# Scores of eleven query blocks in 64x64 tiles instead of 64x32, with new orders for all engines

## The chip, the cores and the metric

The kernel runs on one core of one Trainium2 chip. The metric is the device time of one execution in microseconds (us). TensorE is called PE in the profile (PEld are its weight loads), VectorE is DVE, ScalarE is ACT, GpSimd is POOL and SyncE, which issues the DMAs, is SP.

## What is computed

Four residual layers over a sequence of 2048 tokens of width 448, in bfloat16. Layers 0 and 2 are attention, layers 1 and 3 a gated product. Each attention query looks at eight keys: its own position and the seven positions 2, 4, ..., 14 back.

```python
# layers 0 and 2: 16 heads of 28
q, k, v = split((layernorm(x) @ wqkv))
logits  = sum(q[s] * k[s - 2*w]) * 28**-0.5      # w = 0..7, masked before position 0
x = x + softmax(logits) @ v-window @ wo
# layers 1 and 3: F = 1792
h = layernorm(x)
x = x + ((h @ w_gate) * (h @ w_up)) @ w_down
```

## The kernel before

**Tokens and layout.** Even and odd tokens never meet in the attention, so x is kept with all even tokens first, and the window of eight keys becomes eight neighbours. A head of 28 is padded to 32 rows. All large products run in mode R64 (`MAIN`): PE is cut into two halves of 64 rows, and two products, one in each half, run beside each other (the 64\*128 tiles of the profile).

**Attention.** The queries are cut into 17 blocks: block 0 of 128 queries, the others of 120. Block 0 is a group by itself, the other blocks go two by two, so there are nine groups, g = 0..8, per attention layer. For each group `attn_front` (line 811) does these steps. DVE writes Qz (line 820), two copies of the queries, each with half of the heads set to zero. PE computes the scores S in one burst (line 832): keys are stationary, queries move. A burst of a pair of blocks has 64 products: 4 chunks of heads x 2 blocks x 2 halves of the keys (c) x 2 strips of 32 keys (s\_) x 2 halves of the rows (p). Each loads 32 keys, and streams two copies of 32 or 40 queries. That is mode C32 (`BURST`): tiles of 64 rows by 32 columns, eight of them at once. Then ACT takes the exponential (line 841) in two instructions and DVE masks by a minimum (line 848). `attn_back` (line 852) multiplies by v in a second burst AV, also 64 products of mode C32 (line 866); ACT and DVE evict it (877, 881), `norm` divides (891 to 904), and `y_blocks` multiplies by wo and adds to x (921).

**Gated layers.** `b_chunk` (line 931) takes chunks of 256 or 512 tokens: for each of 14 slices of F a unit of 14 products (G and U of a slice beside each other), ACT copies G (957), DVE multiplies it by U into hT (960), and 14 + 14 products with WD add to x (921). The last 256 tokens use whole-array products (line 972) and smaller adds (976).

**What sets the order.** The program is a list of 1593 operations with dependencies; no planner runs. `ORDER` gives the order of the operations on each engine as literal numbers, and `BANKS` gives the PSUM banks of each PE operation. In the PE list, `548*3/418` means that burst 548 is cut into four pieces, and between the pieces the first three product pairs of operation 418 run as strips of 32 columns (line 351), which is the burst's own mode, so that PE need not change mode for them; a burst that is a number alone stands alone. `24+25/26` puts two bursts ahead of one host. Where ACT, DVE and POOL can do the same copy, the list in which its number stands decides. In `crossed` (line 632) a product group is done in two parts, with the row halves exchanged; the second part waits for the end of the first on PE itself, so the lists normally put other work between the two parts (373 and 374, for example, are the two parts of one v group).

The score bursts are 215 (g 0), 249, 271, 379, 401, 526, 548, 599, 621 in layer 0, and 765 to 1355 in layer 2. The AV bursts are 220, 254, 276, 384, 406, 531, 553, 604, 626, and 770 to 1360.

Of the kernel before, what the change touches and what calls it, by code (L numbers as in the profile page):

```python
# [12 lines left out]
W = 8  # L13
# [15 lines left out]
BURST = "C32"  # L29
MAXALT = 3  # L30
# [63 lines left out]
def grp_nc(g):  # L94
# [21 lines left out]
    ),  # L116
    "act": (
# [12 lines left out]
    ),  # L130
    "dve": (
# [18 lines left out]
    ),  # L150
    "pool": (
        "22 23 24 39 40 18 32 33 25 19 20 28 21 41 42 44 29 26 27 34 35 64 67 68 65 71 73 74 76 36 37 30 43 31 38"
    ),
# [185 lines left out]
def pe_cols(n):  # L339
    return n / 2.4 + 2.6  # L340
# [36 lines left out]
def build(nc, A_x, A_wqkv, A_wo, B_w_gate, B_w_up, B_w_down, out):  # L377
# [22 lines left out]
    qk = sb([128, 2, 4, S], bf, "qk")  # L400
# [11 lines left out]
    Qz = sb([128, NZ, 2, 4, 2 * QB], bf, "Qz")  # L412
# [8 lines left out]
    ps = enter(nc.psum_tensor("ps", [128, 8, 512], dt.float32))  # L421

    sc = Sched()
# [121 lines left out]
    for n in range(4):  # L545
        a, z = 7 * n // 2, 7 * (n + 1) // 2
# [264 lines left out]
    def attn_front(li, g, prio):  # L811
        qbs, nc = grp_qbs(g), grp_nc(g)
        nd = len(qbs)
# [289 lines left out]
```

## Time and profile before

| | |
|---|---|
| three runs | 389.02, 389.04, 389.85 us (median 389.04) |
| profiled execution, whole | 389.22 us |
| its span from first to last instruction | 387.4 us |
| granted PE clock | 0.999 |
| PE busy | 378.5 us, 6442 products and as many weight loads |
| DVE / ACT / POOL busy | 290.9 / 203.1 / 9.2 us |
| L832 (scores), 64\*32 tiles | 1088 products, 89 ns a load, 185 to 208 ns a product by the record |
| L866 (times v), 64\*32 tiles | 1088 products |

A line of the timeline gives the start, the length from the first start to the last end, the engine and source line, out<-in, the PE tile (rows\*columns), the shape and the count; brackets give idle time before it and what ended it. A product's record goes on for some 0.19 us after its operands have been issued, since products are pipelined. So the cost of a group is read from its start to the start of the next group, not from its length. The whole time of the profiled execution is 1.8 us longer than the span: that lies before the first and behind the last instruction.

### The profile page before, as it was taken

To read this page: it belongs to the slowest core of one execution; us is meant where nothing else is said; L and a number is where in the kernel's file an instruction comes from. 1 tells how busy PE (TensorE), PEld (TensorE's weight loads), DVE (VectorE), ACT (ScalarE), POOL (GpSimd) and SP (SyncE) were. 2 spreads that over 40 slices of the span, in tenths; PEclk is the share of its full clock that TensorE was granted. 3 is DMA by queue.
4 is the path that set the end of the run, shared out by engine and by line. 5 is a ranking of instruction groups with operands and counts; after the bars stand their busy time and mean duration, and the time that the engine had idled before them with its cause. 6 is when DMAs were issued, how large, how long until landed. Compare 5 with 4: busy or idle time off the path is not lost.

```text
span 387.4 us, 14498 instructions
## 1 busy us (share of the span) xinstructions
PE 378.5 (98%) x6442; PEld 213.2 (55%) x6442; DVE 290.9 (75%) x643; ACT 203.1 (52%) x386; POOL 9.2 (2%) x39
## 2 busy tenths in 40 slices
PE   7999899999999999999999999999999999999996
PEld 3655468644455544555656667654555544445763
DVE  7988899999974877597877788667997877365332
ACT  5999787565634643355364535446655643044310
POOL 6020000000000000000000000000000000000000
PEclk9999999999999999999999999999999999999999
DMA  7765641800502060122022204300133005030002
GB/s 263 181 159 135 100 116 47 104 12 12 88 17 52 3 96 15 24 44 47 17 31 51 42 2 96 70 14 5 49 48 72 2 2 98 13 83 2 3 25 85
DMA packets 54882, 22.52 MB, mean 58 GB/s; under 512 B 45012, under 2 KB 54820, under 8 KB 54820
## 3 DMA queue, kind: packets, MB, share of 16 engines
q1 hardware_dynamic: 54676, 21.53, 26.7%
q8 instruction: 51, 0.84, 0.9%
q14 instruction: 11, 0.09, 0.1%
q10 hardware_dynamic: 144, 0.06, 0.1%
HBM read 8.54 MB, written 2.71 MB: 29 GB/s over the span
## 4 chain that ended last, share of the span: by engine, by line
PE 93%; DVE 2%; ACT 1%; DMA 1%; SPq 1%; issue 1%; DVEq 0%
PE ps L348 84%; PE ps L351 2%; PE ps L866 2%; PE ps L832 2%; PE ps L972 1%; DMA hT<-in_A_wqkv_dram 1%; ACT E_sb L841 1%; SPq L441 1%; PE ps L614 0%; DVE x_sb L921 0%; DVE hT L960 0%; DVE E_sb L848 0%; ACT g_sb L957 0%; DVE qk L709 0%; DVEq L1052 0%
## 5 line engine op out<-in xcount | busy, mean ns | idle before, releaser
L348 PE MATMUL ps<-xnTb,WGU 64*128 64x512 bf16 (+1 forms) x1926 | 175.5, 333 | 1.0 <-ACT E_sb L841 0.4
L348 PEld LDWEIGHTS ps<-xnTb,WGU 64*128 64x128 bf16 x1926 | 94.0, 94 | 72.3 <-issue 2.3
L957 ACT ACTIVATE g_sb<-ps 128x512 bf16<-128x512 f32 (+1 forms) x140 | 69.4, 509 | 93.6 <-PE ps L348 74.8
L960 DVE TENSOR_TENSOR hT<-g_sb,ps 128x512 bf16<-128x512 bf16 (+1 forms) x140 | 77.4, 575 | 37.1 <-ACT g_sb L957 34.3
L348 PE MATMUL ps<-WD,hT 64*128 64x448 bf16 x800 | 81.7, 350 | 0.2 <-DVE x_sb L921 0.2
L348 PEld LDWEIGHTS ps<-WD,hT 64*128 64x128 bf16 x800 | 38.4, 94 | 34.5 <-DVE x_sb L921 0.5
L348 PE MATMUL ps<-xnTa,WQK 64*128 64x512 bf16 (+1 forms) x498 | 54.4, 353 | 0.1
L921 DVE TENSOR_TENSOR x_sb<-x_sb,ps 128x448 bf16<-128x448 bf16 x62 | 36.7, 612 | 14.6 <-PE ps L348 14.5
L841 ACT ACTIVATE E_sb<-ps,shift_sb 128x1024 bf16<-128x1024 f32 (+1 forms) x36 | 37.1, 1069 | 17.2 <-PE ps L832 17.2
L579 DVE BATCH_NORM_STATS2 st<-x_sb 128x6 f32<-128x448 bf16 x64 | 38.4, 617 | 1.0 <-DMA x_sb<-in_A_x_dram 0.4
L600 DVE TENSOR_SCALAR xn_sb<-x_sb,mv,rstd 128x512 bf16<-128x512 bf16 (+1 forms) x64 | 35.3, 567 | 1.7 <-ACT rstd L584 1.3
L348 PEld LDWEIGHTS ps<-xnTa,WQK 64*128 64x128 bf16 x498 | 23.2, 94 | 20.6 <-PE ps L348 0.9
L709 ACT ACTIVATE qk<-ps 128x1024 bf16<-128x1024 f32 (+1 forms) x27 | 24.8, 927 | 13.1 <-PE ps L348 12.8
L348 PE MATMUL ps<-wo_g,oT 64*128 64x448 bf16 x250 | 29.0, 350 | 0.1
L848 DVE TENSOR_TENSOR E_sb<-E_sb,MK 128x1024 bf16<-128x1024 bf16 (+1 forms) x36 | 23.2, 659 | 6.7 <-ACT E_sb L841 6.7
L892 ACT ACTIVATE R_sb<-R_sb 128x480 f32<-128x480 f32 (+1 forms) x34 | 20.2, 600 | 13.1 <-DVE R_sb L891 12.7
L904 DVE TENSOR_TENSOR oT<-O_sb,R_sb 128x480 bf16<-128x480 f32 (+3 forms) x36 | 22.0, 625 | 3.0 <-ACT R_sb L893 2.9
L348 PE MATMUL ps<-WV,xnTa 64*128 64x336 bf16 (+3 forms) x246 | 23.4, 305 | 0.8 <-DMA WV<-in_A_wqkv_dram 0.7
L891 DVE STREAM_SHUFFLE R_sb<-O_sb 128x480 f32<-128x480 f32 (+1 forms) x34 | 23.2, 693 | 0.0
L820 DVE TENSOR_SCALAR Qz<-qk,qmask 128x960 bf16<-128x960 bf16 (+1 forms) x36 | 14.8, 452 | 7.8 <-PE ps L832 4.4
L893 ACT ACTIVATE R_sb<-R_sb 128x480 f32<-128x480 f32 (+1 forms) x34 | 20.3, 603 | 0.4
L348 PEld LDWEIGHTS ps<-wo_g,oT 64*128 64x128 bf16 x250 | 12.1, 94 | 10.9 <-PE ps L348 0.8
(66 smaller groups left out, 214.0 us busy)
## 6 DMA issues: line engine op xcount, KB each, us to landing
out_dram<-x_sb SPq DMA_DIRECT2D x15, 112.0 KB, 1.9
x_sb<-in_A_x_dram SPq DMA_DIRECT2D x3, 448.0 KB, 5.6
hT<-in_A_wqkv_dram SPq DMA_DIRECT2D x4, 224.0 KB, 4.6
WGU<-in_B_w_gate_dram SPq DMA_DIRECT2D x4, 224.0 KB, 4.1
WGU<-in_B_w_up_dram SPq DMA_DIRECT2D x4, 224.0 KB, 3.5
WD<-in_B_w_down_dram SPq DMA_DIRECT2D x2, 448.0 KB, 4.4
WGU<-in_B_w_gate_dram SPq DMA_DIRECT2D x2, 336.0 KB, 4.3
WGU<-in_B_w_up_dram SPq DMA_DIRECT2D x2, 336.0 KB, 5.0
```

The source lines that it names most:

```text
L348: return lambda E: E.matmul(out(), lhs(), rhs(), start=start, stop=stop)
L579: sc.add("dve", one(lambda E, B=B: E.bn_stats(st6[:, B, :], x_sb[:, B, :]), ("bn", li, B)), 525.0, deps=[("x", li - 1, B)] + ([("xn", li - ...
L600: sc.add("dve", one(lambda E, B=B, dst=dst, src=src: E.tensor_scalar(dst, src, mv[:, B, 0:1], rstd[:, B:B + 1], ALU.subtract, ALU.mult), ( ...
L709: return E.activation(dst, src, ACT.Copy) if hasattr(E, "activation") else E.tensor_copy(dst, src)
L841: return E.activation(E_sb[:, slot, 2 * hp:2 * hp + 2, 0:w], ps[:, b0:b0 + 2, 0:w], ACT.Exp, bias=shift_sb[:, 0:1], scale=SCALE)
L848: return E.tensor_tensor(e, e, MK[:, kind, 0:nc].unsqueeze(1).unsqueeze(1).to_broadcast([128, 2, w // nc, nc]), ALU.min)
L891: sc.add("dve", one(lambda E: E.stream_shuffle(R_sb[:, rs, 0:w], O_sb[:, os_, 0:w], [DH] * 32), ("Rs", li, qb)), dve_est(w) + 20.0, deps=[ ...
L893: sc.add("act", one(lambda E: E.activation(R_sb[:, rs, 0:w], R_sb[:, rs, 0:w], ACT.Exp, scale=-1.0), ("R", li, qb)), act_est(w, False), de ...
L904: return E.tensor_tensor(oT[:, :, a % HALF:a % HALF + z - a], O[:, :, a - tok:z - tok], R_sb[:, rs, 0:w].rearrange("p (h n) -> p h n", h=4 ...
L921: sc.add("dve", one(lambda E: E.tensor_tensor(x_sb[:, B, :], x_sb[:, B, :], ps[:, bk[w], 0:D], ALU.add), ("x", li, B)), dve_est(D), deps=[ ...
L957: sc.add("act", one(lambda E, gs=gs, bk=bk: E.activation(g_sb[:, gs, 0:nt], ps[:, bk[0], 0:nt], ACT.Copy), ("G", li, j, fc)), act_est(nt), ...
L960: sc.add("dve", one(lambda E, gs=gs, bk=bk, fc=fc: E.tensor_tensor(hT[:, fc, hs, 0:nt], g_sb[:, gs, 0:nt], ps[:, bk[1], 0:nt], ALU.mult), ...
```

## The change

For groups 0 to 5 of layer 0 (query blocks 0 to 10) the loop over the two strips of 32 keys is dropped: a product loads 64 keys and streams two copies of up to 64 queries (128 columns instead of 64 or 80), in mode C64: tiles of 64 rows by 64 columns, four of them at once. A burst of a pair of blocks has 32 products instead of 64; that of group 0 has 16 instead of 32. The other score bursts and all AV bursts keep their tiles.

All five engine lists and the PSUM banks are new. No operation is added or dropped.

```diff
+WIDE_S = ((0, 0), (0, 1), (0, 2), (0, 3), (0, 4), (0, 5))
...
-        for hc, d, c, s_, p in [(hc, d, c, s_, p) for hc in range(4) for d in range(nd) for c in range(2) for s_ in range(2) for p in range(2)]:
+        wide = (li, g) in WIDE_S
+        KN = 64 if wide else 32
+        for hc, d, c, s_, p in [(hc, d, c, s_, p) for hc in range(4) for d in range(nd) for c in range(2) for s_ in range(64 // KN) for p in range(2)]:
...
-            ks, qs = ck + 64 * c + 32 * s_, cq + 56 * c - tok
+            ks, qs = ck + 64 * c + KN * s_, cq + 56 * c - tok
...
-            lo, hi = max(0, ks - qs - tok), min(nc, ks - qs - tok + 32 + W - 1 + 1)
+            lo, hi = max(0, ks - qs - tok), min(nc, ks - qs - tok + KN + W)
...
-        sc.add("pe", ins, ..., mode=BURST, acquire=bk, prio=prio)
+        sc.add("pe", ins, ..., mode="C64" if wide else BURST, acquire=bk, prio=prio)
...
 ORDER "pe", around groups 3 and 4 of layer 0
-... 573 276 569 570 574 379 373 374 401 302 305 308 384 311 314 288 ...
+... 569 357 370 502 570 276*2/503 379 573 574 373 374 401 305 311 302 384 314 308 320 288 ...
 ORDER "pe", end
-... 1526 1527 1575 1578 1516 1517 1587 1590 1584 1518 1519
+... 1526 1527 1519 1584 1587 1590
```

In the new PE list these bursts stand alone or share a host's strips:

| | before | after |
|---|---|---|
| alone, layer 0 | 215 249 220 254 271 276 379 401 384 526 406 | 215 249 220 271 379 401 384 526 531 |
| alone, layer 2 | 765 924 946 | 765 929 |
| with a host | 22 bursts at 19 hosts | 25 bursts at 22 hosts |
| PE products in all | 6442 | 6314 |

(32 x 5 + 16 = 176 products fewer in the bursts; eight more product pairs of hosts are done as eight strips each, 48 more.) The two parts of a crossed group follow each other directly in five places before (211, 503, 570, 374, 544 directly behind their first parts) and in four after (211, 574, 374, 267). At the end, before, the last PE group is 1518 and 1519, two blocks of 128 tokens that end together; after, it is 1590, half of the columns of one block (128x224). Some copies change engine: of the first weight copies (line 518) one more stands on DVE and fewer on POOL; in layer 0, moves of evictions between ACT and DVE add about 0.8 us to DVE by the durations of their rows. On SP the second half of WV (line 453) is issued one place earlier, and the first of the two small loads for the v columns (line 463) behind three weight loads.

More of the change, by code (lines that the diff above doesn't have):

```diff
@@ L102 @@
     "pe": (
[13 rows of a table removed]
[13 rows of a table added]
     ),
     "act": (
[12 rows of a table removed]
[12 rows of a table added]
     ),
     "dve": (
[18 rows of a table removed]
[18 rows of a table added]
     ),
     "pool": (
-        "22 23 24 39 40 18 32 33 25 19 20 28 21 41 42 44 29 26 27 34 35 64 67 68 65 71 73 74 76 36 37 30 43 31 38"
+        "24 28 25 20 18 29 21 32 39 30 26 27 19 33 35 40 31 41 22 42 70 36 64 23 44 66 34 37 38 43 71 76 78"
     ),
     "sp": (
[5 rows of a table removed]
[5 rows of a table added]
     ),
@@ L826, in attn_front @@
         ins, cols = [], []
-        for hc, d, c, s_, p in [(hc, d, c, s_, p) for hc in range(4) for d in range(nd) for c in range(2) for s_ in range(2) for p in range(2)]:
+        wide = (li, g) in WIDE_S
+        KN = 64 if wide else 32
+        for hc, d, c, s_, p in [(hc, d, c, s_, p) for hc in range(4) for d in range(nd) for c in range(2) for s_ in range(64 // KN) for p in range(2)]:
             ck, nk, cq, nq = qb_info(qbs[d])
-            ks, qs = ck + 64 * c + 32 * s_, cq + 56 * c - tok
+            ks, qs = ck + 64 * c + KN * s_, cq + 56 * c - tok
             b, h = e_at(nd, hc, d, p)
-            lo, hi = max(0, ks - qs - tok), min(nc, ks - qs - tok + 32 + W - 1 + 1)
+            lo, hi = max(0, ks - qs - tok), min(nc, ks - qs - tok + KN + W)
             ins.append((lambda E, hc=hc, c=c, s_=s_, p=p, b=b, h=h, ks=ks, qs=qs, lo=lo, hi=hi: E.matmul(
-                ps[64 * c + 32 * s_:64 * c + 32 * s_ + 32, bk[b], 2 * nc * h:2 * nc * (h + 1)].rearrange("p (a n) -> p a n", a=2)[:, :, lo:hi], qk[64 * p:64 * p + 64, 0, hc, ks:ks + 32],
-                Qz[64 * p:64 * p + 64, zs, :, hc, qs + lo:qs + hi], start=True, stop=True, tile_position=(64 * p, 64 * c + 32 * s_)), None))
+                ps[64 * c + KN * s_:64 * c + KN * s_ + KN, bk[b], 2 * nc * h:2 * nc * (h + 1)].rearrange("p (a n) -> p a n", a=2)[:, :, lo:hi], qk[64 * p:64 * p + 64, 0, hc, ks:ks + KN],
+                Qz[64 * p:64 * p + 64, zs, :, hc, qs + lo:qs + hi], start=True, stop=True, tile_position=(64 * p, 64 * c + KN * s_)), None))
             cols.append(hi - lo)
         ins[-1] = (ins[-1][0], [("S", li, q) for q in qbs])
-        sc.add("pe", ins, sum(pe_cols(2 * n) for n in cols) / 8, deps=deps + [prev, ("Qz", li, g)], mode=BURST, acquire=bk, prio=prio)
+        sc.add("pe", ins, sum(pe_cols(2 * n) for n in cols) / (4 if wide else 8), deps=deps + [prev, ("Qz", li, g)], mode="C64" if wide else BURST, acquire=bk, prio=prio)
         for hp in range(2):
```

126 rows, old and new, of tables (BANKS, ORDER) are left out of this document.

## Prediction, made before the changed kernel was run

> **What bounds the kernel now.** I read the busy times first, then the chain that ended last.
>
> ```profile
> PE 378.5 (98%) x6442; PEld 213.2 (55%) x6442; DVE 290.9 (75%) x643; ACT 203.1 (52%) x386; POOL 9.2 (2%) x39
> ...
> PE 93%; DVE 2%; ACT 1%; DMA 1%; SPq 1%; issue 1%; DVEq 0%
> ```
>
> PE carries the chain, so time is won only where PE idles, is held up, or works at less than its rate. The timeline of PE gives the price of a group as the distance from its start to the next start. 14 products of 64x512 cost 1.51 us, of 64x448 1.32, of 64x256 0.76, and these prices repeat to 0.01 us wherever nothing waits. Whatever exceeds them can be listed. Around groups 2 to 4 of layer 0:
>
> ```profile
> 38.82 0.68 PE L832 MATMUL ps<-Qz,qk 64*32 64x64 bf16 x64
> 39.44 0.82 PE L348 MATMUL ps<-xnTa,WQK 64*128 64x512 bf16 x6
> ...
> 46.65 0.54 PE L832 MATMUL ps<-Qz,qk 64*32 64x64 bf16 x47
> 48.09 0.26 PE L832 MATMUL ps<-Qz,qk 64*32 64x64 bf16 x17 [0.90 <-issue]
> 48.28 1.41 PE L348 MATMUL ps<-WV,xnTa 64*128 64x336 bf16 x14
> 49.62 0.68 PE L832 MATMUL ps<-Qz,qk 64*32 64x64 bf16 x64
> 50.72 1.90 PE L348 MATMUL ps<-xnTb,WGU 64*128 64x256 bf16 x31 [0.41 <-ACT E_sb L841]
> 52.84 0.81 PE L348 MATMUL ps<-xnTb,WGU 64*128 64x256 bf16 x11 [0.22 <-issue]
> ```
>
> An undisturbed burst of 64 takes 0.62 us (38.82 to 39.44). The one at 46.65 takes 1.63: it stops after 47 products for something called issue. The third unit of WGU from 52.25 stops too (1.34 us to the next group instead of 0.76 + 0.09), and so does the burst at 61.17 (1.01). The restarts at 48.09, 52.84 and 62.17 are PE instructions number 1729, 1985 and 2497, whole multiples of 256 apart. Instructions come in packets: in the stretch from 44 to 64 us the DMA view counts
>
> ```profile
> q8 instruction: 5, 0.08, 1.5%
> ```
>
> 16 KB each; 51 in all for 12,884 loads and products, about 253 instructions a packet. In the trace's records the packet ahead of each of the three stops starts 2.24, 2.48 and 2.35 us before PE goes on. I read them as waits for instructions, price 1.02 + 0.48 + 0.40 = **1.9 us**. Priced undisturbed, the 256 instructions before those stops take 2.4, 3.8 and 4.3 us; as they ran, 3.6, 4.8 and 4.9.
>
> **The change, part by part** (in the profiled execution, 389.22 us).
>
> *1. The wide bursts themselves.* No row shows a 64\*64 tile. Within the burst of 38.82 the first 32 products start within 0.14 us; after a hole of 0.09 the others come every 8.4 ns. The 32-product bursts at 155.48 (S, to 155.74) and 28.64 (AV, to 28.89) take 0.26. So the late half of a burst is paced by the supply of instructions, the early half is not, and 32 wide products should lie in the early half. They then run at the rate of the streams: 128 columns at the rate of 64x512 (216 ns) are 56 ns; 32 / 4 tiles = 8 rounds, last start after 7 x 56 = 0.39, then 0.13 to the next mode (39.307 to 39.432 in the records) and 0.02 for the longer last stream: 0.54. Ends: 0.26, if only the number of products counts; 1.26, if each of 8 rounds also waits out a load of 89 ns (0.54 + 0.71). I take 0.55, since a whole 64\*128 stream of 64x512 shows loads beside products of the same half, and 0.26 and 0.62 lie around it. Five bursts at -0.07, group 0 (16 products, 4 rounds, 0.17 + 0.15 = 0.32 against 0.26) +0.06: **-0.3**. ACT's exponentials behind them (1.07 us each) and Qz start no more than that earlier.
>
> The Trainium skill speaks against this (TensorEngine Tiling (Array Packing), Restrictions): column tiling switches fast weight load off; TensorE: Matmul & The Clock Gate, LDWEIGHTS, prices a load by its columns, P / 1.2, an estimated 53 ns for 64. By it, unhidden, a burst would take 0.54 + 8 x 0.053 = 0.97, and this part would be +2 instead of -0.3. The trace has 89 ns for 32 columns and 94 for 128, latencies mostly, so it does not decide.
>
> *2. Waits for instructions.* In the new order, at the same row prices, the 256 instructions up to numbers 1729, 1985, 2241 and 2497 take 4.7, 4.1, 6.4 and 4.1 us. Before, 3.6 to 4.9 was what a packet needed there. The first and worst stop should go, one or two short ones may stay; I keep 0.4: **-1.5** (ends -1.9 and 0; a stop elsewhere, as from 25.7 to 28.9 with 3.3 us for 256, would use it up).
>
> *3. Bursts with a host's strips.* Alone, an AV or S burst costs 0.62, 0.09 for the change of mode before it and 0.01 behind: 0.72. With two strip sets:
>
> ```profile
> 106.63 0.92 PE L348 MATMUL ps<-wo_g,oT 64*128 64x448 bf16 x8
> 107.48 0.27 PE L866 MATMUL ps<-E_sb,v_sb 64*32 64x64 bf16 x21
> ...
> 108.37 2.44 PE L348 MATMUL ps<-WD,hT 64*128 64x448 bf16 x24
> 110.65 0.92 PE L348 MATMUL ps<-wo_g,oT 64*128 64x448 bf16 x8
> ```
>
> 107.48 to 110.65 is 3.17 with two WD groups of 1.32 inside: 0.52, and 0.09 ahead: 0.61. With three sets (121.82 to 123.59, less 1.32, and 0.10 ahead) 0.55. So 254, 276 and 406 win 0.11, 0.11, 0.15; 531, now alone, loses 0.15; in layer 2, 924, 946 and 1157 win 0.07, 0.16 and 0.09, and 929 loses 0.11: **-0.4**.
>
> *4. Crossed parts.* 373 and 374 together take 1.34 (48.28 to 49.62); apart, such parts take 0.43 and 0.57, and 0.09 is the change of mode: 0.25 for standing together. One such place fewer: **-0.2**.
>
> *5. The end.*
>
> ```profile
> 378.75 0.39 DVE L976 TENSOR_TENSOR x_sb<-x_sb,ps 128x224 bf16<-128x224 bf16 x1 [3.67 <-PE ps L972]
> ...
> 381.29 2.82 PE L348 MATMUL ps<-WD,hT 64*128 64x448 bf16 x28
> 384.14 1.15 DVE L921 TENSOR_TENSOR x_sb<-x_sb,ps 128x448 bf16<-128x448 bf16 x2 [1.83 <-PE ps L348]
> ```
>
> Today two adds of 448 columns (1.15) stand behind the last product, then an output DMA (1.9). After the change one add of 224 columns (0.39) does: -0.76. PE also changes to whole-array products once instead of there and back: -0.09. DVE now adds blocks 10 and 11 before 12 and 13, whose bank 6 the group 1587 needs; three adds of 0.57 fit under 1584's 2.65. **-0.8**.
>
> *6. The head.* WV's second half comes one issue (0.5) earlier; PE waits 0.66 for it now. The fifth block's normalization stands behind two weight copies that wait for their loads, and the last weight copy is POOL's (0.56) instead of DVE's (0.27). The two pull against each other; **0** (ends -0.4 and +0.4). The delayed small load for v is wanted only at 21.5 us by copies that wait for PE.
>
> *7. What is late next.* Parts 1 to 5 give -3.2, of which -1.9 falls before 70 us, where DVE has little left:
>
> ```profile
> 48.00:78.00 30.00, 28.82 (x787) 20.88 (x789) 28.29 (x68) 22.16 (x44) 0.00 (x0) 1.00 0.46 88
> 78.00:107.00 29.00, 28.93 (x418) 13.92 (x420) 27.30 (x56) 17.79 (x33) 0.00 (x0) 1.00 0.24 39
> ```
>
> The columns are PE, PEld, DVE, ACT, POOL. DVE is busy 55.6 of 59 us, and gets 0.8 more. If PE is to gain 1.9 here, DVE must find 2.7 in 3.4 us of gaps, which do not all lie well. One bank wait is plain in the order: 573 now follows the AV burst 276 by one host and one wide burst, and takes the bank that 279 (DVE, behind ACT's and DVE's evictions) frees, about 0.4 us too late. I charge **+1.3** for 573 and for DVE together (ends +0.4 and +2.7).
>
> Sum: -0.3 - 1.5 - 0.4 - 0.2 - 0.8 + 0 + 1.3 = -1.9: 387.3 against the profiled 389.22. That execution lay 0.2 above the median of the runs shown, so I say **387.2 us**; alone, this case reaches from 386.0 to 388.2.
>
> **Rivals.**
> - *DVE takes over* the whole stretch to 107 us: part 7 costs 2.7. -0.5: 388.6. For it: 94% busy; against: PE, not DVE, ended nearly all waits there.
> - *Instructions are late elsewhere*: part 2 gives nothing. -0.4: 388.7. For it: DMA is 46 to 61% busy up to 78 us and packets queue; against: 256 instructions then need 4 us and more.
> - *The other side: loads stand between the products of a tile.* In the late half of a 64\*32 burst a tile comes round every 67 ns for a stream of some 33, which leaves up to 33 ns for a load of 32 columns, so 67 for 64: 8 x 0.067 on 0.55 is 1.08 a burst, +0.46 x 5 and +0.3 for group 0 instead of -0.3: part 1 is +2.6, the sum +1.0: 390.1. Slower begins at about 0.9 a burst. For it: no such tile in the trace; against: AV bursts of 64 columns (0.61) and S bursts of 64 and 80 (0.62) cost alike, so supply paces them. The two sections of the Trainium skill named in part 1 describe this mechanism; by their figure the sum would be about +0.4, 389.6.
>
> **How the numbers follow.** Forecast 0.62, DVE 0.14, instructions 0.10, loads 0.14. About 0.2% (0.8 us) can be told from no change, so same is 388.3 to 389.8. The forecast case is faster throughout; the first two rivals straddle the border (faster 0.08, same 0.14, slower 0.02); the third is slower (0.13) or same (0.01). Faster 0.70, same 0.15, slower 0.15. The range runs from 386.0, where waits for instructions and the head give all they can, to 389.2, which takes in the first two rivals and leaves out the third.
>
> **What would show it.** Wide bursts of 0.5 to 0.6 us from start to next start (part 1); no idle on issue between 44 and 64 us (2); DVE near 95% busy from 48 to 105 us, and PE waiting for it no more than 1.3 us in all (7); 128x224 as the last add with nothing but its output behind (5). I am wrong if wide bursts exceed 0.9, or if PE idles on DVE for over 2 us before 107.

## The result and the profile after

| | before | after |
|---|---|---|
| median of the runs | 389.45 us (4 runs, 389.02 to 389.91) | 386.39 us (4 runs, 386.11 to 387.48) |
| profiled execution | 389.22 us, span 387.4 | 386.11 us, span 384.4 |
| PE's first start, first score burst | 1.78, 21.52 us | 1.29, 21.04 us |
| start of PE's last group to the end of the span | 4.79 us | 3.9 us |

The ratio is 0.9927 with a 95% interval from 0.9902 to 0.9952: faster by 0.7%. 387.2 was forecast, with a range from 386.0 to 389.2, and the measured time lies in that range, near its lower end. Between the two profiled executions 1.9 us less were forecast and 3.1 less were measured. The sum is no further off because its two largest misses lie on opposite sides: the gain from instructions was 0.75 us smaller than forecast, and the loss that was charged for DVE 1.1 us smaller. That they cancel in part is luck. First the busy times of the changed kernel, from its page:

```profile
PE 378.5 (98%) x6314; PEld 213.0 (55%) x6314; DVE 288.6 (75%) x641; ACT 202.2 (53%) x390; POOL 8.3 (2%) x37
```

PE has 128 products fewer and is busy for as long as before: what was won is time without products, at the start, at the end and in stops. The timeline of PE (start, duration, engine, line, operation, operands, tile, shape, count) shows wide bursts undisturbed:

```profile
23.97 0.64 PE L835 MATMUL ps<-Qz,qk 64*64 64x128 bf16 x32
24.54 0.82 PE L349 MATMUL ps<-xnTa,WQK 64*128 64x512 bf16 x6
...
46.02 0.64 PE L835 MATMUL ps<-Qz,qk 64*64 64x128 bf16 x32
46.69 1.18 PE L349 MATMUL ps<-xnTa,WQK 64*128 64x256 bf16 x14
```

From 23.97 to 24.54 are 0.57 us, against 0.62 of a burst of 64 (part 1 of the prediction). In the single records of this burst four products start together, 0.08 us later the next four, and from then on four every 0.056 us. That is the rate of the streams which part 1 assumed, though each of its loads lasts some 0.1 us by its record. The second takes 0.67: the group behind it, 573, waits 0.10 for its bank, which is the wait that part 7 priced at 0.4. The burst at 46.02 is the one that stopped at 48.09 in the kernel before; it does not stop. But in the AV burst of block pair 2, which now shares its host's strips, there is a stop that was not there:

```profile
29.19 0.42 PE L352 MATMUL ps<-xnTa,WQK 64*32 64x512 bf16 x5
29.29 0.33 PE L869 MATMUL ps<-E_sb,v_sb 64*32 64x64 bf16 x4
30.58 0.27 PE L869 MATMUL ps<-E_sb,v_sb 64*32 64x64 bf16 x18 [0.96 <-issue]
30.78 1.04 PE L349 MATMUL ps<-xnTa,WQK 64*128 64x512 bf16 x12
```

Four products of the last 22, then nothing, then the other 18; "issue" again. The restart at 30.58 is PE instruction number 961 (loads, products and PE's few semaphore instructions counted in the order of the trace), and 1729, 1985 and 2497 of the kernel before are 3, 4 and 6 times 256 further. The last packet of instructions ahead of it began 2.72 us earlier. This stop costs 1.16; it is the only one of its kind in the trace.

DVE, in the windows view (PE, PEld, DVE, ACT, POOL):

```profile
48.00:75.00 27.00, 26.39 (x686) 18.82 (x682) 26.61 (x66) 21.88 (x44) 0.00 (x0) 1.00 0.48 98
```

It is busy 26.61 of 27 us up to 75, as feared, and yet the view of waits lists none of PE for DVE from 22 to 107 us. The end, on PE and on DVE:

```profile
376.49 5.50 PE L975 MATMUL ps<-WD,hT 128*128 128x448 bf16 x42
```

```profile
382.04 0.39 DVE L979 TENSOR_TENSOR x_sb<-x_sb,ps 128x224 bf16<-128x224 bf16 x1 [0.96 <-PE ps L975]
```

One add of 224 columns is the last, as in part 5.

### The profile page after: what moved, and what is told of

It reads as the page before. It is cut to its first block, busy times and chain, and to the rows that moved or that the text cites. A ratio compares the mean times of both kernels' runs of the same rounds, so it can differ in the third digit from the quotient of the medians.

```text
span 384.4 us, 14257 instructions
## 1 busy us (share of the span) xinstructions
PE 378.5 (98%) x6314; PEld 213.0 (55%) x6314; DVE 288.6 (75%) x641; ACT 202.2 (53%) x390; POOL 8.3 (2%) x37
## 4 chain that ended last, share of the span: by engine, by line
PE 94%; DVE 3%; ACT 2%; issue 1%
PE ps L349 84%; PE ps L352 3%; PE ps L869 2%; PE ps L835 2%; PE ps L511 2%; PE ps L975 1%; ACT qk L710 1%; DVE hT L963 1%; DVE st L580 1%; ACT E_sb L844 1%; PE ps L615 0%; DVE xn_sb L601 0%; ACT R_sb L895 0%; DVE E_sb L851 0%; DVE R_sb L894 0%
## 5 line engine op out<-in xcount | busy, mean ns | idle before, releaser
L963 DVE TENSOR_TENSOR hT<-g_sb,ps 128x512 bf16<-128x512 bf16 (+1 forms) x140 | 78.7, 574 | 42.0 <-ACT g_sb L960 39.9
L349 PE MATMUL ps<-WD,hT 64*128 64x448 bf16 x784 | 79.8, 349 | 0.0
L349 PEld LDWEIGHTS ps<-WD,hT 64*128 64x128 bf16 x784 | 37.3, 94 | 33.1 <-DVE hT L963 0.5
L349 PE MATMUL ps<-xnTa,WQK 64*128 64x512 bf16 (+1 forms) x490 | 52.7, 352 | 0.3 <-ACT qk L710 0.2
L349 PEld LDWEIGHTS ps<-xnTa,WQK 64*128 64x128 bf16 x490 | 22.4, 94 | 21.1 <-DVE hT L963 0.9
L710 ACT ACTIVATE qk<-ps 128x1024 bf16<-128x1024 f32 (+1 forms) x27 | 24.0, 913 | 7.1 <-PE ps L349 6.9
L880 ACT ACTIVATE O_sb<-ps 128x512 f32<-128x512 f32 (+3 forms) x21 | 10.9, 546 | 23.0 <-PE ps L869 22.9
```

The source lines that it names most:

```text
L349: return lambda E: E.matmul(out(), lhs(), rhs(), start=start, stop=stop)
L710: return E.activation(dst, src, ACT.Copy) if hasattr(E, "activation") else E.tensor_copy(dst, src)
L963: sc.add("dve", one(lambda E, gs=gs, bk=bk, fc=fc: E.tensor_tensor(hT[:, fc, hs, 0:nt], g_sb[:, gs, 0:nt], ps[:, bk[1], 0:nt], ALU.mult), ...
```

## Experiments

Two theories were to be told apart. **S (supply):** most of the gain hangs on where the 256-instruction packets of PE end: a stop falls where a packet's instructions pass faster than the next packet comes, wherever that is in the program. **O or P (orders, place):** the gain belongs to the orders or tiles themselves, and a stop to the burst in which it is seen. "Cost" of a stop below is the time from the group's start to the next start less that of the same group undisturbed. None of these kernels changes what is computed; the warm-up products whose count is changed are read by nobody.

**Orders alone.**

```diff
-WIDE_S = ((0, 0), (0, 1), (0, 2), (0, 3), (0, 4), (0, 5))
+WIDE_S = ()
```

> The new orders and banks with all score bursts left in 64x32 tiles (64 products). Theory S (the wide tiles pay through the supply of instructions, hardly through their own length): priced by the rows of before, the 256 PE instructions up to numbers 1729, 1985 and 3265 now take 2.3, 3.3 and 2.1 us, where 3.6 to 4.9 were needed for a packet; waits of 3 to 4.5 us in all on issue at these numbers, and +0.2 for the bursts: 389 to 391 us, slower than the changed kernel by 2.5 to 4. Rival O (the new orders carry the gain, the tiles nothing): within 0.5 us of the changed kernel, 386.4 to 386.9.

Measured 389.31 us (12 runs), ratio 1.0002 [0.9988, 1.0016]. On the face of it the orders bring nothing; the trace says something else. Four stops, of 0.68 at 24, 0.54 at 72, 0.53 at 204 and 1.94 at 260 us, stand in it, 3.7 us in all, and the largest is in layer 2:

```profile
260.87 0.28 PE L869 MATMUL ps<-E_sb,v_sb 64*32 64x64 bf16 x18
263.00 0.25 PE L869 MATMUL ps<-E_sb,v_sb 64*32 64x64 bf16 x14 [1.86 <-issue]
263.18 0.39 PE L349 MATMUL ps<-xnTa,WQK 64*128 64x512 bf16 x2
```

263.00 is number 9665, 34 packets behind 961. From 256 to 264 us DMA is busy 4%, so it is not the DMA's load that makes a packet late. The four restarts have their packet's start 2.76, 2.55, 2.20 and 2.62 us behind them. The time is the one that S gave, but not the places: of the three numbers that S named (1729, 1985 and 3265) only 3265 shows a stop.

**Tiles alone** (the kernel before with the loop and the mode of the wide bursts):

```diff
+WIDE_S = ((0, 0), (0, 1), (0, 2), (0, 3), (0, 4), (0, 5))
...
+        wide = (li, g) in WIDE_S
+        KN = 64 if wide else 32
```

> The old orders and banks with the first eleven query blocks in 64x64 tiles. Theory S: no 256 instructions take less than 4.1 us at row prices, so the three stops of before (1.9 us) go and none comes in their place; 0.2 from the bursts themselves: 2 us below before, 387.0 to 387.8. Rival O: no more than the 0.2 of the bursts, 389.0 to 389.3.

Measured 392.33 us (6 runs, one of them an outlier of 1372.62), ratio 1.0063 [1.0047, 1.0080]: a miss for S as I had written it. The three old stops are gone as forecast, the wide bursts take 0.57; but 0.92, 1.79 and 1.27 us are lost at 205, 260 and 295 us, in layer 2, whose products nobody touched. All three restart at a packet's end (numbers 7105, 9153, 10433). Removing 176 products ahead had moved the packets' ends in all that follows, and I had looked for them in layer 0 only.

**Ninety-six instructions ahead of all others**, in the kernel before (a warm-up product of 512 columns becomes four of 128):

```diff
+WSPLIT = (4, 16)
...
-        sc.add("pe", one(lambda E, n=n: E.matmul(ps[:, n % NBK if n < NBK else wb[0], :], warm[:, 0:128], warm, start=True, stop=True), ("warm", n)), ...
+        k = 512 // (WSPLIT[0] if n < WSPLIT[1] else 1)
+        sc.add("pe", [(lambda E, n=n, c=c, k=k: E.matmul(ps[:, n % NBK if n < NBK else wb[0], c:c + k], warm[:, 0:128], warm[:, c:c + k], start=True, stop=True), ("warm", n) if c + k == 512 else None) for c in range(0, 512, k)], ...
```

> The old kernel, but each of the 16 warm-up products of 512 columns is split into four of 128 columns: the same columns, 48 products and 96 PE instructions more, all before the first real work. Theory S: the stops follow the instruction number, not the place in the work: stops at numbers 1985 and 2241 (256 instructions in 2.5 and 3.4 us), none behind the 47th product of burst 379 and none in the third unit of WGU where they were; sum of waits 1.5 to 2.7, time within 1 us of before. Rival P (something in burst 379 or its neighbours stops PE, an eviction or a DMA): the stops stay at the same products as before.

Measured 391.43 us (6 runs), ratio 1.0047 [1.0032, 1.0062]. The stops at 48.09, 52.84 and 62.17 are gone; others stand at the new ends of packets, 0.66 at 50.28 (number 1985, as forecast), 0.46 at 206.9 and 1.69 at 263.7. The work and its order are the same, so a stop does not belong to a burst. The time is a miss for S all the same: it was to stay within 1 us of before and is 2 us above it, because the stops in layer 2 were not looked for. The other way round, the three kernels below that keep the count (the end alone, twice, and the load) stop again at 1729, behind the same 47 products, and at 1985, with 0.5 to 1.1 us between the records. None of them stops at 2497. There the profile of the kernel before names DVE, so the 0.40 us of that place are the least certain of the three.

**The end alone, first attempt** (the last groups, DVE's adds and the output DMAs in the new order, two banks changed):

```diff
 ORDER "pe", end
-1526 1527 1575 1578 1516 1517 1587 1590 1584 1518 1519
+1526 1527 1516 1517 1575 1578 1518 1519 1584 1587 1590
```

> The old kernel with its last PE groups reordered as in the change (1518 and 1519 ahead of 1584, 1587 and 1590), the adds and outputs behind them likewise, and two bank numbers. All theories: 0.76 for one add of 224 columns in place of two of 448 behind the last product, 0.09 for one change of mode fewer: 0.85 below before, 388.4 to 388.8. If the end is bound by the output transfers instead: no change.

Measured 390.48 us (12 runs), ratio 1.0026 [1.0017, 1.0035]. 388.4 to 388.8 had been expected. The end became shorter by 0.89, but my own order of the groups ahead of it put a wait of two microseconds in:

```profile
373.92 2.82 PE L348 MATMUL ps<-WD,hT 64*128 64x448 bf16 x28 [1.94 <-DVE hT L960]
```

The bank for 1516 comes free only when DVE's multiplies are done, which stand behind its adds. It decides nothing on the end; the mended kernel is below.

For the next four I marked on each trace every stretch of 256 instructions that passes in under about 3.4 us (4 at most in layer 0), for every possible shift of the count, over the whole program.

**The changed kernel with 24 instructions more ahead** (twelve warm-ups of two halves), the shift at which hardly any such stretch is left; here and in the next two the edit is that of the kernel with 96, with another first line:

```diff
+WSPLIT = (2, 12)
```

> The changed kernel; twelve of its warm-up products of 512 columns are split into two of 256, so that 24 more instructions for PE lie ahead of all others, and every point at which a packet of 256 ends comes 24 instructions earlier in the work. Nothing else moves. Where a packet's 256 instructions pass in less than about 3.4 us, the trace of the kernels so far shows a stop. Theory S (a stop falls where a packet's end meets a dense stretch, so its place in the count decides): in the changed kernel's trace such stretches cost about 1.2 us (the stop at 30.58 above all); with 24 instructions more, the stretches from end to end are all over 3.4 us, so the stop at 30.58 goes (joined burst 254 with 497 at about 0.6 instead of 1.72) and 385.0 to 385.8 us are left. Theory P (the stop belongs to that joined burst and its neighbours): it stays at 1.7, and the time at 386.2 to 386.7.

Measured 385.34 us (4 runs, 384.96 to 385.38), ratio to the kernel before 0.9888 [0.9874, 0.9903]; the fastest of all, and what S expected (385.0 to 385.8; P: 386.2 to 386.7). The joined burst takes 0.56 over its parts instead of 1.72, and no packet's end shows a stop. The same rows:

```profile
29.09 0.42 PE L353 MATMUL ps<-xnTa,WQK 64*32 64x512 bf16 x5
29.19 0.40 PE L871 MATMUL ps<-E_sb,v_sb 64*32 64x64 bf16 x22
```

Twelve products more, and over 1 us less.

**The changed kernel with 96 instructions more**, a bad shift:

```diff
+WSPLIT = (4, 16)
```

> The changed kernel; sixteen warm-up products of 512 columns split into four of 128, 96 more instructions for PE ahead of all others. Theory S: the ends of packets now enclose dense stretches at about 71 us, 203 us and 259 us (256 instructions in some 1.4 us of work each), with a stop of 0.5 to 2.0 us at each as in the kernel with the orders alone; 388.8 to 391.3 us, so that the whole gain is gone, with no change of the work or its order. Theory P (orders and tiles carry the gain): 386.2 to 386.8 us.

Measured 388.53 us (12 runs, 387.55 to 391.56), ratio 0.9984 [0.9964, 1.0003]: two thirds of the gain are lost in the median, a little less than S expected. The profiled execution took 391.01; in it stops of 0.8, 1.1 and 2.0 us stand at the three forecast places:

```profile
71.97 0.25 PE L837 MATMUL ps<-Qz,qk 64*32 64x64 bf16 x7
72.82 0.23 PE L837 MATMUL ps<-Qz,qk 64*32 64x64 bf16 x9 [0.61 <-issue]
...
204.46 0.25 PE L837 MATMUL ps<-Qz,qk 64*32 64x64 bf16 x9
205.63 0.22 PE L837 MATMUL ps<-Qz,qk 64*32 64x64 bf16 x7 [0.93 <-issue]
...
261.57 0.28 PE L871 MATMUL ps<-E_sb,v_sb 64*32 64x64 bf16 x18
263.72 0.30 PE L871 MATMUL ps<-E_sb,v_sb 64*32 64x64 bf16 x14 [1.87 <-issue]
```

Not all of the loss is stops. The first score burst started 0.7 us late (21.75), and behind the longest stop the granted clock, the third column from the end in this row of the windows view, is down to half:

```profile
264.50:266.00 1.50, 1.50 (x10) 0.46 (x8) 1.46 (x5) 1.16 (x2) 0.00 (x0) 0.50 0.07 16
```

It stays there for 3.4 us, and the group at 264.36, 14 products of 64x512, takes 2.79 us instead of 1.51. Stops of 3.9, a start of 0.7 and some 1.4 for the clock, less the 1.16 that the changed kernel loses at 30.58, make up the 4.9 us by which this execution is longer. The two slowest of the 12 runs (391.01 and 391.56) are the only ones with a mean granted clock of 0.996, and the three slowest of the orders alone (390.16 to 391.19) have 0.996 as well.

**The kernel before with 36 more**, the shift at which the marks left least:

```diff
+WSPLIT = (4, 6)
```

> The kernel before; six warm-up products of 512 columns split into four of 128, 36 more instructions for PE ahead of all others. Theory S: the stops of 1.02, 0.48 and 0.40 us at 40.1, 44.2 and 54.6 us go, with small ones left near 47 and 50 us; 387.4 to 388.4 us. Theory P: 389.0 to 389.9 us, as the kernel before.

Measured 388.18 us (5 runs), ratio 0.9965 [0.9952, 0.9977], as S expected (387.4 to 388.4; P: 389.0 to 389.9). No stop at a packet's end is left in its trace.

**The tiles alone with 108 more:**

```diff
+        k = 512 // (8 if n < 2 else 4 if n < 15 else 2)
```

> The kernel before with the wide tiles alone, as the second experiment had it (392.33 us), and 108 more instructions for PE ahead of all others (two warm-up products in eight parts, thirteen in four, one in two), which may cost up to 0.5 us at the start of the first burst, to be read from the trace. Theory S: that kernel's stops of 0.92, 1.79 and 1.27 us at 205, 260 and 295 us go, or most of them; 388.3 to 389.8 us. Theory P (the wide tiles, in orders not made for them, cost 3 us of themselves): 392 to 392.8 us.

Measured 388.69 us (11 runs), ratio 0.9973 [0.9961, 0.9984]. The three stops of layer 2 are gone and with them 3.6 us; P falls. About 1 us is lost at 48 us in this execution, in the crossed parts 373 and 374:

```profile
48.90 0.74 PE L349 MATMUL ps<-WV,xnTa 64*128 64x336 bf16 x8 [0.67 <-PE ps L349]
```

Their costs over the row prices are 0.85 and 0.50, against 0.24 and 0.13 with narrow tiles and the same orders. But the trace of the tiles alone, with the same orders and the same wide tiles, has 0.24 and 0.30 there, so this is not a price of wide tiles in the old orders. It is not at a packet's end either, and what PE waited for was not settled.

**The orders alone with 176 more** (ten of the warm-up products also get weights of 32 columns):

```diff
+        k, m = (64, 32) if n < 10 else (128, 128)
```

> The kernel with the new orders and banks and no wide tiles, as the first experiment had it (389.31 us), with 176 more instructions for PE ahead of all others: of its sixteen warm-up products ten are split into eight of 64 columns with weights of 32 columns, six into four of 128. Its trace showed stops of 0.68, 0.54, 0.53 and 1.94 us over the usual cost at 24, 72, 204 and 260 us, 3.7 in all; moved by 176 instructions only the stretch near 46 us is still dense (256 instructions in about 2.7 us). Theory S, in which the orders gain as much as the whole change and lose it again to the packets: 385.6 to 387.2 us (389.3 less 3.7, up to 0.7 left at 46 us, up to 0.9 at the start of the first burst). Its rival: the orders need the wide tiles, and gain nothing without them; 388.5 to 389.5 us.

Measured 390.85 us (12 runs, 386.79 to 392.12), ratio 1.0017 [0.9993, 1.0042]: outside what S expected, and within neither theory's reach. The first burst starts only at 22.55, after a wait of 1.14 us for DVE, and the profiled execution (392.12) has stops at four places, of which I had marked one:

```profile
293.87 0.29 PE L870 MATMUL ps<-E_sb,v_sb 64*32 64x64 bf16 x22
296.04 0.23 PE L870 MATMUL ps<-E_sb,v_sb 64*32 64x64 bf16 x10 [1.88 <-issue]
```

All lie at packets' ends (numbers 961, 1217, 1985, 10945), but the length of the stretch alone did not foretell them. The experiment failed to isolate the orders.

**The end alone, mended** (the groups ahead of it and the banks left as they were):

```diff
-1516 1517 1587 1590 1584 1518 1519
+1516 1517 1518 1519 1584 1587 1590
```

> The kernel before with its end in the new order alone: the last products of blocks 12 and 13 ahead of those of 14 and 15, the narrow column part of 15 last; banks as before, so that the wait of 2.1 us which the first such kernel had at 370.5 us goes. If the end is a term of its own: last start of PE to the end of the span 3.9 us instead of 4.8, one change of the tiles' mode fewer (0.09); 388.2 to 388.8 us. If another chain ends last as soon as this one is short: 389.0 us or more.

Measured 388.98 us (8 runs) against 389.74, ratio 0.9977 [0.9967, 0.9987]: 0.76 less, and 0.2 above the range that was expected. The trace ends with one narrow add, 3.9 us after the start of PE's last group:

```profile
384.52 0.39 DVE L976 TENSOR_TENSOR x_sb<-x_sb,ps 128x224 bf16<-128x224 bf16 x1 [0.95 <-PE ps L972]
```

**The load of V's second half earlier:**

```diff
 ORDER "sp"
-0 1 2 7 8 5 9 6 3 4
+0 1 2 7 8 9 5 6 3 4
```

> The kernel before with one load moved: the load of the second half of the weights for V is issued ahead of one of the weights for Q and K, as in the changed kernel. If the wait of 0.66 us for those weights at 8.2 us is what the start loses: no wait there, the first burst at about 21.1 us instead of 21.5; 388.7 to 389.3 us, if the rest of the kernel moves with it. If the start is bound by the norms' transposes or the Q and K weights: first burst still at 21.4 to 21.6, time as before or up to 0.3 us longer.

Measured 389.83 us (11 runs), ratio 1.0004 [0.9995, 1.0013]. The wait for the weights at 8.2 us is gone, as expected, but the first burst starts at 21.89, not at 21.1: now PE waits for the norms, 0.41 us here and 0.49 at 11.46:

```profile
6.74 0.40 PE L610 MATMUL ps<-ident,xn_sb 128*128 128x128 bf16 x4 [0.41 <-DVE xn_sb L600]
```

So this load alone is not what the changed kernel's start gained by.

**Shift, end and load together**, in the kernel before (the edits of the last two, and in the warm-ups:)

```diff
+        k = 512 // (4 if n < 6 else 1)
```

> The kernel before with three things at once: 36 more instructions for PE ahead of all others (388.18 us alone), the end in the new order, the load of V's second half earlier; no wide tile, and every order between start and end as before. If the terms add up: 388.2 less 0.9 for the end and 0 to 0.45 for the start, 386.8 to 387.3 us; what is then left to the changed kernel at its better alignment (385.34 us) is 1.5 to 2 us of orders within the span and of wide tiles. If they hide behind each other: 387.6 us or more.

Measured 387.64 us (6 runs), ratio 0.9954 [0.9938, 0.9970]. That is just outside what was expected if the terms add (386.8 to 387.3) and at the edge of the rival (387.6 or more); but that sum had taken 0.9 for the end and up to 0.45 for the load. With the load at nothing, the measured single differences (1.43 from the shift, 0.76 from the end) give 389.74 - 2.19 = 387.55, so by these the terms do add. The profiled execution, 389.60, is the slowest of the six. It has two stops, of 0.9 us at number 961 and of 1.4 at 1729, that the kernel with the shift alone did not show, though the instructions of PE are the same up to there; at such stretches (3.6 to 4 us) a stop comes in some executions and not in others.

## Why the prediction came out right, step by step

The time came out inside the range, but two of the steps failed, in parts 2 and 7, and one gain, in part 6, had no source in the prediction.

| part | predicted | in the traces |
|---|---|---|
| 1 wide bursts | -0.3 | -0.4 |
| 2 waits for instructions | -1.5 | -0.75 |
| 3, 4, 7 joined bursts, crossed parts, DVE | +0.7 | -0.4 |
| 5 end | -0.8 | -1.0 |
| 6 head | 0 | -0.5 |
| sum | -1.9 | -3.1 |

(The last column is worked out from the starts of the groups in the two profiled executions, 389.22 and 386.11; the change of mode is counted with the end, and 0.1 of the sum lies outside the spans. Parts 3, 4 and 7 are what is left between the first score burst and the end once parts 1 and 2 are taken off.)

- *Part 1* held. Five bursts take 0.57 instead of 0.62. Group 0 was charged 0.06 and gained 0.15 (0.54 instead of 0.69), because the wait for DVE behind it is gone. The rival of loads between products would have needed 1.08. The Trainium skill's rule (TensorEngine Tiling (Array Packing), Restrictions) that column tiling switches fast weight load off, with the load's price in TensorE: Matmul & The Clock Gate, LDWEIGHTS, gave an estimate of 0.97 for a burst; the trace disagrees with adding that price to the streams. Neither section says that a load cannot run beside the streams; to add it was the prediction's own step.
- *Part 2* is mis-sized, by 0.75. The three stops went (-1.9), and no idle on issue is left between 44 and 64 us, but 1.16 came back at 30.58. The prediction named the stretch from 25.7 to 28.9 as one that could use the gain up, and kept 0.4 for all such places. Apart from that one it priced only packets between 44 and 64 us, and took 3.6 to 4.9 us as what a packet needs there, which a rival put down to busy DMA; the stop at 260 us in the orders alone came with DMA at 4%. It also never asked for layer 2, where other counts lose up to 2 us; that the changed kernel loses nothing there is the luck of its count.
- *Part 7* is mis-sized, by about 1.1 the other way. The bank wait of 573 was priced at 0.4 and costs 0.10; DVE is as full as forecast (98% up to 75 us) and does not hold PE up. Joined bursts and crossed parts cost what the rows of before gave (0.61 with two strip sets, 0.44 to 0.55 with three, 0.23 to 0.24 for a crossed pair), so the sum of 3 and 4 stands, and the +1.3 is what failed: an engine that is nearly full was priced as a wait of PE, and that wait did not come.
- *Part 5* held: 0.89 less behind PE's last start and one change of mode; 0.76 by itself on the chip.
- *Part 6* missed 0.5, on the good side and for a reason it did not have. The load that it named gains nothing by itself. The warm-up products begin at 1.29 instead of 1.78, because DVE writes their data before another constant. That this is the carrier is argued, not tested: kernels with the old start put their first burst at 21.52 to 21.97, those with the new start at 20.95 to 21.11, but for the two whose warm-ups were split furthest (21.75 and 22.55).
- *Is the gain the tiles' or the orders'?* At the best shift of each, before is at 388.18 and the changed kernel at 385.34: 2.8 us have nothing to do with stops. In their profiled executions (spans of 386.4 and 383.2) 0.9 us lie ahead of the first burst, 0.9 behind the start of PE's last group, and 1.4 between the two: 0.4 from the wide bursts, 0.1 from one change of mode fewer, 0.6 by the row prices of parts 3 and 4, and 0.3 that no run separates. Only the end was tested by itself (0.76). The tiles alone, without stops, gain nothing (388.69, with the loss at 48 us in the one execution that was profiled). The orders alone, less their stops, come to 388.8 - 3.7 = 385.1 in their profiled execution, which would make them the whole gain, but the kernel meant to show that free of stops did not. So theory S explains why versions landed 1 to 4 us apart, and not where the net gain of this change comes from.

## What to carry to other kernels

When instructions are taken out of or put into a program, number them: a packet's stretch of 256 of PE's instructions that passes quickly, anywhere behind the edit, is a place for a stop, and the sum of a local change can be moved by several microseconds far away from it. In the fourteen traces here, with the stop itself taken off, all 7 stretches of under 2 us ended in a stop, 10 of 22 from 2 to 3.5 us, 11 of 50 from 3.5 to 4.45, and 3 of some 600 longer ones. Before an order is judged slower or faster, shift its count by a few dozen harmless instructions at the start; here that turned 386.39 into 385.34 and into 388.53. An engine at 98% busy is a reason to look for waits, not a price by itself.

## What the runs showed of the hardware

- In eleven of the fourteen profiled executions 31 stops of 0.3 to 2.1 us (from one record of PE to the next) end exactly at a number 193 + 256 k of PE's instructions, 2.2 to 2.95 us after the start of the last packet of 16 KB ahead of them, which is the k-th. At none of some 680 such numbers, with a stop or without, does PE go on sooner than 2.2 us after the start of its packet, if the k-th packet of the queue is the one that begins there, as at the 31 stops. When a packet starts varies (at the stops, between 0.4 us before and 3.5 us after the first instruction of the 256 ahead), and why was not found; so the same stretch stops in some executions only.
- Two kernels with several stops scatter widely: 387.55 to 391.56 and 386.79 to 392.12. Those without any reach from 384.96 to 385.38, 388.12 to 388.97 and 387.89 to 389.22. Stops alone do not make the scatter: the kernel before, with three, stays within 389.02 to 390.32 in 26 runs.
- Behind one stop of 1.9 us the granted clock fell to 0.5 for 3.4 us; behind two others as long (at 263 us in the orders alone, at 296 us in the orders with 176 more) it stayed at 1.00.
- A dense joined burst (24 products of a host as strips among the 128 of two AV bursts) takes 256 instructions in some 1.4 us, so that a packet's end inside it costs 1.7 to 2.0 us in layer 2, with DMA nearly idle.
- Warm-up products of 512 columns start every 0.425 us and change to 0.213 at 4.7 us in one execution, at 5.1 in two others, and only after 6 us in others, while the page gives a granted clock of 1.00 for all these slices. The same code at the start put the first burst at 21.52 us with the change at 4.7 and at 21.97 with a change after 6.9, but at 21.52 also with a change at 6.0, so this is not shown to set the start.
